# Where the polynomial's q and g's first part are made in the last block of the first MLP, and how wide the steps of a weight conversion are

## The chip, the cores and the metric

One core of a Trainium2 chip runs the whole program. The metric is the device time of one execution in microseconds (us); lower is better. Several executions are timed and their median counts; one more execution is taken with the hardware profiler.

## What is computed

The reference chains three parts. A recurrence with a 48 x 48 state per head (4 batches, 8 heads, 768 steps) gives 3072 tokens of width 384. The first MLP (384 to 2048 to 384) follows, and then a second MLP (384 to 1024 to 384) with a softmax-gated norm between its two products.

```python
x = attn_out.transpose(0, 2, 1, 3).reshape(3072, 384)
h = x @ w_in;  x = (h - np.tanh(h)) @ w_out               # first MLP
h = x @ w_in2; solu = h * softmax(h)                      # second MLP
out = ((solu - mean) / np.sqrt(var + 1e-06) * g_ln) @ w_out2
```

The weights come as 64-bit floats and are turned into 32-bit ones on the chip.

## The kernel before

Each 32-bit operand of the two MLPs is held as a rounded high part and a low part, so that one product takes three matmul passes (low by high, high by low, high by high).

**The first MLP** runs over 6 blocks of 512 tokens (index i, `NB` is 6) and, in each, over 16 tiles of 128 hidden columns (index m). I count the tiles through: tile s is block s // 16, so block 0 holds tiles 0 to 15 and the last block tiles 80 to 95. `part1` (line 328) makes one tile. Nine matmuls (L334) fill a PSUM bank `hp`; the pool of these has two banks, so the matmuls of tile s+2 need the bank of tile s free. Then h - tanh(h) is made as an odd polynomial: ScalarE squares hp into t (L339), VectorE makes y = hp * t (L340), ScalarE makes the inner square p from t (L342), VectorE finishes y (L344) from p and y, ScalarE raises a range flag from t and writes its unused main result to q (L345), y is rounded into g's first part (L347 on ScalarE or L349 on GpSimd), and GpSimd makes the second part, y minus the first (L350). In block 0 p is the bank hp itself and the rounding is ScalarE's L347; in the other blocks p is q, an SBUF tile, and the rounding is GpSimd's L349.

`part2` (line 353) takes g two tiles later: nine matmuls (L357) add it into three PSUM banks x2p. At the end of a block ScalarE copies these out (L362), and the result goes through DRAM to the second MLP.

**The conversion** (`convert`, line 109) turns a pair of 64-bit weight rows into 768 32-bit columns. ScalarE scales the low words (L118), VectorE shifts and masks the high words (L125), adds the sign bits (L126) and adds the low words (L127); ScalarE scales half by the norm's weights (L129, second MLP only) and rounds (L130), GpSimd makes the low part (L131). L125 and L126 run in two steps of 384 columns each. For the first MLP (`conv_a`, during block 0) the intermediate a lies in PSUM; for the second (`conv_b`, eight conversions, issued in the last block) there is no bank to spare, and a lies in the SBUF tile x, of which there are two buffers. `conv_b` of k is called at every second tile of the last block (line 551), but two of them start earlier and the rest is pulled ahead.

**Order.** The Python order is not the order on the engines: a planner sorts every engine's instructions by simulated time when the program is built. Each engine then runs its queue in that order, and an instruction that waits holds up all that stand behind it on its engine. Until the last block starts, the recurrence for later tokens is mixed into the same queues. After the last block the second MLP follows (L412, L446, L457); one half of its first product's weights is ready in the last block, and its first matmuls run there.

The lines that matter are quoted.

```python
p = hp if i == 0 else q                                   # L341
nc.scalar.activation(p, t, AF.Square, bias=..., scale=F_S)
v.scalar_tensor_tensor(y, p, F_E, y, ALU.add, ALU.mult)   # L344
```

Of the kernel before, what the change touches and what calls it, by code (L numbers as in the profile page):

```python
# [19 lines left out]
NT, DM, FF, FF2 = 3072, 384, 2048, 1024  # L20
# [5 lines left out]
NB = NT // BLK  # L26
# [29 lines left out]
class Kern:  # L56
# [52 lines left out]
    def convert(self, pool, raw, hi, lo, scale=None, bank=None):  # L109

        nc, v = self.nc, self.nc.vector
        flat = raw.rearrange("p i f two -> p (i f) two")
        H_, L_ = flat[:, :, 1], flat[:, :, 0]
        x = pool.tile([128, 2 * DM], U32, tag="cv_x", name="cv_x")
        xf = x.bitcast(F32)
        nc.scalar.activation(L_, L_, AF.Copy, scale=2.0**-29)  # L118
        for i in range(2):
            s = slice(i * DM, (i + 1) * DM)  # L120
            if bank is None:
                a = x[:, s]
            else:
                a = bank.tile([128, 4, C], F32, tag="a", name="cv_a").rearrange("p j t -> p (j t)")[:, 0:DM].bitcast(U32)
            v.tensor_scalar(a, H_[:, s], 3, 0x3FFFFFF8, ALU.logical_shift_left, ALU.bitwise_and)  # L125
            v.scalar_tensor_tensor(x[:, s], H_[:, s], 0xC0000000, a, ALU.bitwise_and, ALU.bitwise_or)  # L126
        v.tensor_tensor(x, x, L_, ALU.add)  # L127
        if scale is not None:
            nc.scalar.activation(xf[:, DM:], xf[:, DM:], AF.Copy, scale=scale)  # L129
        nc.scalar.copy(hi, xf)  # L130
        nc.gpsimd.tensor_tensor(lo, xf, hi, ALU.subtract)  # L131
# [196 lines left out]
    def part1(self, i, m):  # L328
        nc, v, g = self.nc, self.nc.vector, self.nc.gpsimd
        hp = self.ps_h.tile([128, BLK], F32, tag="h", name="hp")  # L330
        xs = self.xs[i % 2]
        seq = [(a, b, j) for j in range(KM) for a, b in ((1, 0), (0, 1), (0, 0))]
        for n, (a, b, j) in enumerate(seq):
            self.mm(hp, self.wa[:, a, m, j * 128:(j + 1) * 128], xs[:, b, j], start=n == 0, stop=n == len(seq) - 1)  # L334
        t = self.gp.tile([128, BLK], F32, tag="t", name="t")
        q = self.gp.tile([128, BLK], F32, tag="q", name="q")
        y = self.gp.tile([128, BLK], F32, tag="y", name="y")
        gs = self.gs.tile([128, 2, BLK], F32R, tag="g", name="g")
        nc.scalar.activation(t, hp, AF.Square)  # L339
        v.tensor_tensor(y, hp, t, ALU.mult)  # L340
        p = hp if i == 0 else q  # L341
        nc.scalar.activation(p, t, AF.Square, bias=self.c_fsb, scale=F_S)  # L342
        col = 2 * NU + i * NM + m
        v.scalar_tensor_tensor(y, p, F_E, y, ALU.add, ALU.mult)  # L344
        self.last_act = nc.scalar.activation(q, t, AF.Relu, bias=self.c_t2, accum_out=self.flags[:, col:col + 1])  # L345
        if i == 0:
            nc.scalar.copy(gs[:, 0], y)  # L347
        else:
            g.tensor_scalar(gs[:, 0], y, 1.0, 1.0, ALU.mult, ALU.mult)  # L349
        g.tensor_tensor(gs[:, 1], y, gs[:, 0], ALU.subtract)  # L350
        return gs
# [419 lines left out]
```

## Time and profile before

| what | us |
|---|---|
| median of 3 timed executions | 837.1 (836.93 to 837.52) |
| the profiled execution's own time | 833.47 |
| its span, first to last instruction | 831.7 |
| TensorE (PE) busy | 779.4 |
| VectorE (DVE) busy | 548.6 |
| ScalarE (ACT) busy | 490.5 |
| GpSimd (POOL) busy | 377.2 |

PE runs the matmuls, PEld loads their weights. Times in the trace count from the span's start. A row of the timeline gives the start, the length, the engine, the line, the operation, output and inputs, their shapes, how many instructions were merged into the row, and in brackets the idle time of the engine before it and what ended that. A granted clock of 1.00 is TensorE's full 2.4 GHz, 0.50 is 1.2 GHz. The last block's matmuls run from about 520 us to 603 us.

### The profile page before, as it was taken

How to read it: one execution, taken by the hardware profiler on the slowest of the kernel's cores; microseconds unless marked ns; L12 is line 12 of the kernel's file. 1: busy time of each engine (PE TensorE's matmuls, PEld its weight loads, DVE VectorE, ACT ScalarE, POOL GpSimd, SP SyncE). 2: the span in 40 equal slices, each digit the busy share in tenths (PEclk: the TensorE clock that was granted, in tenths of full speed). 3: DMA queues.
4: the chain of work that ended last, by engine and by line, in shares of the span. 5: the costliest groups of instructions: out<-in, count | busy, mean ns of one | idle time of the engine just before them, and what ended most of it. 6: DMA issues, size and time to landing. Idle time of an engine off the chain costs nothing.

```text
span 831.7 us, 13450 instructions
## 1 busy us (share of the span) xinstructions
PE 779.4 (94%) x4706; PEld 649.1 (78%) x4706; DVE 548.6 (66%) x997; ACT 490.5 (59%) x928; POOL 377.2 (45%) x360
## 2 busy tenths in 40 slices
PE   3778988999999999999999999889989999999996
PEld 2656766778878888888888788667879999999996
DVE  4688889666664566565556763895287577667763
ACT  3436776677666767677677765655445454445442
POOL 3544765655555655556556465676412111111110
PEclk9988998899999999999999999999999999999998
DMA  9966567435455554463434220410021111111101
GB/s 164 166 107 127 138 146 151 136 100 115 90 120 114 125 108 105 107 157 81 119 100 130 82 81 25 140 50 2 10 67 39 48 39 48 39 48 39 48 29 33
DMA packets 151309, 74.32 MB, mean 89 GB/s; under 512 B 107328, under 2 KB 142784, under 8 KB 151232
## 3 DMA queue, kind: packets, MB, share of 16 engines
q1 hardware_dynamic: 151232, 73.37, 37.0%
q8 instruction: 39, 0.64, 0.3%
q14 instruction: 38, 0.31, 0.1%
HBM read 61.54 MB, written 9.44 MB: 85 GB/s over the span
## 4 chain that ended last, share of the span: by engine, by line
PE 75%; DVE 11%; DMA 4%; issue 2%; POOL 2%; ACT 2%; SPq 2%; DVEq 0%; ACTq 0%; POOLq 0%
PE hp L334 19%; PE x2p L357 18%; PE o L457 12%; PE h L412 11%; PE qk L254 3%; PE tp L218 3%; DVE cv_x L126 2%; PE tt L446 2%; DVE cv_x L127 2%; PE y L296 2%; PE y L293 2%; DMA raw<-in_moe_w_out_dram 1%; DVE cv_x L125 1%; DMA raw<-in_moe_w_in_dram 1%; PE kt L260 1%
## 5 line engine op out<-in xcount | busy, mean ns | idle before, releaser
L357 PE MATMUL x2p<-g,wa 128*128 128x512 f32 x864 | 226.4, 401 | 9.0 <-POOL g L350 4.6
L334 PE MATMUL hp<-xs,wa 128*128 128x512 f32 x864 | 225.8, 403 | 6.7 <-POOL wa L131 3.2
L334 PEld LDWEIGHTS hp<-xs,wa 128*128 128x128 f32 x864 | 162.5, 192 | 45.2 <-POOL wa L131 3.7
L357 PEld LDWEIGHTS x2p<-g,wa 128*128 128x128 f32 x864 | 160.3, 191 | 46.0 <-POOL g L350 6.3
L350 POOL TENSOR_TENSOR g<-y,g 128x512 fp32r<-128x512 f32 x96 | 129.3, 1347 | 17.4 <-ACT g L347 9.7
L340 DVE TENSOR_TENSOR y<-hp,t 128x512 f32<-128x512 f32 x96 | 66.2, 689 | 106.6 <-ACT t L339 103.6
L457 PE MATMUL o<-wb,ts 128*128 128x384 f32 x576 | 110.0, 341 | 1.0 <-DVE ts L448 1.0
L345 ACT ACTIVATE q<-t,cst 128x512 f32<-128x512 f32 x96 | 69.5, 724 | 68.1 <-DVE y L344 67.8
L412 PE MATMUL h<-wb,x2s 128*128 128x512 f32 x432 | 103.8, 392 | 2.8 <-DVE so L432 2.4
L349 POOL TENSOR_SCALAR g<-y 128x512 fp32r<-128x512 f32 x80 | 53.9, 674 | 114.8 <-DVE y L344 111.4
L457 PEld LDWEIGHTS o<-wb,ts 128*128 128x128 f32 x576 | 100.5, 188 | 2.9 <-DVE ts L448 1.3
L412 PEld LDWEIGHTS h<-wb,x2s 128*128 128x128 f32 x432 | 80.6, 188 | 19.8 <-issue 3.0
L339 ACT ACTIVATE t<-hp 128x512 f32<-128x512 f32 x96 | 56.6, 591 | 44.8 <-PE hp L334 44.6
L437 POOL TENSOR_TENSOR st<-st,cst 128x1 f32<-128x1 f32 x24 | 13.5, 563 | 136.2 <-DVE st L436 134.8
L344 DVE SCALAR_TENSOR_TENSOR y<-q,y 128x512 f32<-128x512 f32 x80 | 65.4, 818 | 10.6 <-ACT q L342 5.6
L342 ACT ACTIVATE q<-t,cst 128x512 f32<-128x512 f32 x80 | 57.7, 722 | 2.0
L435 ACT ACTIVATE e<-so 128x1024 f32<-128x1024 f32 x24 | 25.4, 1059 | 49.4 <-DVE so L434 49.4
L425 DVE TENSOR_REDUCE st<-h 128x1 f32<-128x1024 f32 x24 | 29.4, 1224 | 28.6 <-PE h L412 27.1
L428 DVE TENSOR_REDUCE part<-e 128x32 f32<-128x1024 f32 x24 | 29.3, 1220 | 27.9 <-ACT e L427 27.9
L218 PE MATMUL tp<-ident,rkw 128*128 128x128 f32 x264 | 41.9, 292 | 6.0 <-DMA rkw<-in_w_dram 5.7
L402 POOL TENSOR_TENSOR x2s<-x2s 128x384 fp32r<-128x384 f32 x24 | 24.4, 1018 | 48.3 <-ACT x2s L401 40.0
L131 POOL TENSOR_TENSOR wa<-cv_x,wa 128x768 fp32r<-128x768 f32 x16 | 29.4, 1838 | 35.3 <-ACT wa L130 35.3
(114 smaller groups left out, 1211.1 us busy)
## 6 DMA issues: line engine op xcount, KB each, us to landing
raw<-in_moe_w_out_dram SPq DMA_DIRECT2D x48, 384.0 KB, 4.0
raw<-in_moe_w_in_dram SPq DMA_DIRECT2D x64, 144.0 KB, 3.2
raw<-in_moe_w_in_dram SPq DMA_DIRECT2D x16, 384.0 KB, 3.1
rkw<-in_w_dram SPq DMA_DIRECT2D x24, 192.0 KB, 4.3
rkw<-in_r_dram SPq DMA_DIRECT2D x24, 192.0 KB, 4.5
rkw<-in_k_dram SPq DMA_DIRECT2D x24, 192.0 KB, 3.9
vt<-in_v_dram SPq DMA_DIRECT2D x24, 192.0 KB, 4.4
x2d<-x2o SPq DMA_DIRECT2D x18, 256.0 KB, 2.2
```

The source lines that it names most:

```text
L218: self.nc.tensor.transpose(p[:, j], self.rkw[u % 2][:, i, 2 * j:2 * j + 2, :], self.ident)
L334: self.mm(hp, self.wa[:, a, m, j * 128:(j + 1) * 128], xs[:, b, j], start=n == 0, stop=n == len(seq) - 1)
L339: nc.scalar.activation(t, hp, AF.Square)
L340: v.tensor_tensor(y, hp, t, ALU.mult)
L342: nc.scalar.activation(p, t, AF.Square, bias=self.c_fsb, scale=F_S)
L344: v.scalar_tensor_tensor(y, p, F_E, y, ALU.add, ALU.mult)
L345: self.last_act = nc.scalar.activation(q, t, AF.Relu, bias=self.c_t2, accum_out=self.flags[:, col:col + 1])
L349: g.tensor_scalar(gs[:, 0], y, 1.0, 1.0, ALU.mult, ALU.mult)
L350: g.tensor_tensor(gs[:, 1], y, gs[:, 0], ALU.subtract)
L357: self.mm(self.x2p[d], self.wa[:, a, m, sl], gs[:, b], start=m == 0 and n == 0, stop=m == NM - 1 and n == 2)
L412: self.mm(p[:, f], xs[:, a, j], self.wb[:, b, 4 * f:4 * f + 4, j * 128:(j + 1) * 128], start=q == 0, stop=q == 8)
L457: self.mm(p, ts[:, a, k], self.wb[:, b, k, DM:], start=q == 0, stop=q == 3 * NM2 - 1)
```

## The change

In the last block, as in block 0 before, L342 writes its result into the bank hp in place of the SBUF tile q, L344 reads it from there, and g's first part is rounded by ScalarE (L347) in place of GpSimd (L349). In the conversion for the second MLP the two steps of 384 columns become one of 768: one L125 and one L126 in place of two of each. The conversion for the first MLP is unchanged.

```diff
-        for i in range(2):
-            s = slice(i * DM, (i + 1) * DM)
+        n = 1 if bank is None else 2
+        for i in range(n):
+            s = slice(i * 2 * DM // n, (i + 1) * 2 * DM // n)
             if bank is None:
-                a = x[:, s]
+                a = x
             else:
                 a = bank.tile([128, 4, C], F32, tag="a", name="cv_a").rearrange("p j t -> p (j t)")[:, 0:DM].bitcast(U32)
...
-        p = hp if i == 0 else q
+        ends = i in (0, NB - 1)
+        p = hp if ends else q
         nc.scalar.activation(p, t, AF.Square, bias=self.c_fsb, scale=F_S)
...
-        if i == 0:
+        if ends:
             nc.scalar.copy(gs[:, 0], y)
         else:
             g.tensor_scalar(gs[:, 0], y, 1.0, 1.0, ALU.mult, ALU.mult)
         g.tensor_tensor(gs[:, 1], y, gs[:, 0], ALU.subtract)
```

## Rows read from the trace of the kernel before

**Rows 1.** Busy by stretch: length, then PE, PEld, DVE, ACT, POOL, granted clock, DMA.

```profile
528.00:540.00 12.00, 9.04 (x35) 6.14 (x35) 11.76 (x12) 8.93 (x17) 8.51 (x6) 1.00 0.64 221
552.00:570.00 18.00, 13.99 (x51) 10.19 (x50) 14.89 (x16) 9.73 (x18) 13.19 (x11) 0.91 0.01 1
...
570.00:597.00 27.00, 27.00 (x120) 22.31 (x119) 10.47 (x15) 14.76 (x29) 13.59 (x15) 1.00 0.00 1
...
558.00:560.00 2.00, 2.00 (x6) 1.52 (x6) 2.00 (x2) 0.62 (x1) 2.00 (x2) 0.50 0.00 0
```

**Rows 2.** Waits of the matmuls by what ended them, 515 to 600 us.

```profile
PE x2p L357 <- POOL g L350: 4.4, 3, 3.2
```

**Rows 3.** Timeline of PE in the last block.

```profile
525.82 2.37 PE L334 MATMUL hp<-xs,wa 128*128 128x512 f32 x9
...
557.66 5.27 PE L357 MATMUL x2p<-g,wa 128*128 128x512 f32 x15 [3.19 <-POOL g L350]
563.23 2.33 PE L334 MATMUL hp<-xs,wa 128*128 128x512 f32 x9 [0.30 <-DVE y L340]
...
588.44 2.20 PE L334 MATMUL hp<-xs,wa 128*128 128x512 f32 x9
```

**Rows 4.** Timeline of DVE in the last block.

```profile
526.55 0.61 DVE L125 TENSOR_SCALAR cv_x<-raw 128x384 uint32<-128x384 uint32 x2
527.09 0.68 DVE L344 SCALAR_TENSOR_TENSOR y<-q,y 128x512 f32<-128x512 f32 x1
...
530.99 1.75 DVE L344 SCALAR_TENSOR_TENSOR y<-q,y 128x512 f32<-128x512 f32 x1
...
535.59 1.02 DVE L126 SCALAR_TENSOR_TENSOR cv_x<-raw,cv_x 128x384 uint32<-128x384 uint32 x2
536.74 0.96 DVE L127 CUSTOM_DVE_ANT_0 cv_x<-raw,cv_x 128x1536 uint16<-128x1536 uint16 x1
...
538.40 1.75 DVE L344 SCALAR_TENSOR_TENSOR y<-q,y 128x512 f32<-128x512 f32 x1
...
552.89 1.43 DVE L126 SCALAR_TENSOR_TENSOR cv_x<-raw,cv_x 128x384 uint32<-128x384 uint32 x2
...
555.72 2.11 DVE L125 TENSOR_SCALAR cv_x<-raw 128x384 uint32<-128x384 uint32 x2
...
563.28 0.69 DVE L344 SCALAR_TENSOR_TENSOR y<-q,y 128x512 f32<-128x512 f32 x1
...
584.01 0.69 DVE L344 SCALAR_TENSOR_TENSOR y<-q,y 128x512 f32<-128x512 f32 x1
```

**Rows 5.** Timeline of POOL in the last block.

```profile
537.75 1.85 POOL L131 TENSOR_TENSOR wb<-cv_x,wb 128x768 fp32r<-128x768 f32 x1 [2.30 <-ACT wb L130]
...
555.11 1.16 POOL L349 TENSOR_SCALAR g<-y 128x512 fp32r<-128x512 f32 x1 [1.66 <-DVE y L344]
556.24 2.72 POOL L350 TENSOR_TENSOR g<-y,g 128x512 fp32r<-128x512 f32 x2
```

**Rows 6.** Lines on their own: count, then min/median/max ns, first and last start.

```profile
L344 DVE SCALAR_TENSOR_TENSOR y<-q,y x80: 677/693/1752, 177.0 to 596.3; 128x512 f32<-128x512 f32 x80
...
L344 DVE SCALAR_TENSOR_TENSOR y<-hp,y x16: 673/682/692, 77.3 to 169.8; 128x512 f32<-128x512 f32 x16
...
L342 ACT ACTIVATE hp<-t,cst x16: 667/692/702, 76.6 to 169.0; 128x512 f32<-128x512 f32 x16
...
L347 ACT CAST g<-y x16: 600/616/632, 80.7 to 170.6; 128x512 fp32r<-128x512 f32 x16
...
L349 POOL TENSOR_SCALAR g<-y x80: 610/620/1184, 177.9 to 597.1; 128x512 fp32r<-128x512 f32 x80
```

**Rows 7.** Waits of the matmuls by what ended them, block 0, 76 to 176 us.

```profile
PE hp L334 <- DVE y L344: 2.7, 1, 2.7
PE x2p L357 <- ACT g L347: 2.4, 1, 2.4
```

**Rows 8.** Timeline of ACT in the last block.

```profile
548.29 0.62 ACT L129 ACTIVATE cv_x<-cv_x,gl 128x384 f32<-128x384 f32 x1 [4.56 <-DVE cv_x L127]
```

## The prediction

> **What bounds the kernel now.** I read the busy time by stretch first, because the change touches only the last block and the conversions that run in it. What a reader should see there is that TensorE has nearly no gaps where the last block runs alone (27.00 us busy of 27.00 from 570 to 597 us) and has gaps only while the conversions run beside it: 12.00 - 9.04 = 2.96 us from 528 to 540 and 18.00 - 13.99 = 4.01 us from 552 to 570 [rows 1]. From 540 to 552 it has none. That is 6.97 us of idle TensorE, and it is all that this change can win directly.
>
> A second loss hangs on the first. After the longest wait, 3.19 us, fifteen matmuls took 5.27 us [rows 3]; nine take 2.20 us elsewhere including the end of the last [rows 3], so fifteen would take about 3.6. The granted clock read 0.50 from 558 to 560 us, so the lower level of 1.2 GHz [rows 1]. That is about 1.7 us more. **The ceiling** of the change is thus 6.97 + 1.7 = 8.7 us.
>
> Then I read who ends the gaps: in 515 to 600 us the second-part subtraction on GpSimd, L350, ends 4.4 us of them, one of 3.2 us [rows 2]. Then I followed this one back on the engines' timelines. L350 of tiles 84 and 85 ran together only at 556.24, behind L349 of tile 85 at 555.11, which waited for VectorE's L344 of tile 85 [rows 5]. VectorE is what is full there: 11.76 of 12.00 us from 528 to 540 [rows 1]. Much of that is not work. L344 took 1.75 us twice, beginning at 530.99 and at 538.40, where its median is 0.693 [rows 4, 6]; the second of these began while GpSimd's L131 ran from 537.75 to 539.60, and lasted 0.55 us beyond it [rows 4, 5]. L125 of two steps took 2.11 us against 0.61, and L126 of two steps 1.43 us against 1.02 [rows 4]. So the chain is: VectorE is held while GpSimd runs, L344 comes late, g comes late, TensorE waits.
>
> **The change part by part.**
>
> *L344 reads hp.* The form that reads q and y, both in SBUF, goes up to 1752 ns; the form that reads hp never took over 692 ns in 16 instances, though fourteen conversions, each with its L131 on GpSimd, run in block 0 [rows 6]. So I take the stretch out of the two long ones: 2 x (1.75 - 0.69) = 2.1 us of VectorE's queue.
>
> *The rounding leaves GpSimd.* Sixteen L349 of 0.62 us [rows 6], 9.9 us, go from GpSimd and become sixteen L347 of 0.616 us, 9.9 us, on ScalarE. VectorE stood behind L349 in at least two places: L126 at 552.89 was 1.43 - 1.02 = 0.4 us longer, and L125 at 555.72 began 0.55 us before the L349 from 555.11 ended [rows 4, 5]. Together 1.0 us. On ScalarE there is room: it is busy 8.93 of 12.00 and 9.73 of 18.00 us in the two stretches [rows 1]. I cost its 9.9 us at nothing; the cover is this idle time, and what it costs when the cover is gone is a rival below.
>
> *Whole steps.* Two L126 of 384 columns took 1.02 us, and one pass over all 768 columns, L127, took 0.96 [rows 4]. A whole-step L126 is not in the trace; L127 is its nearest row, and the saving 0.06 us. For L125 I take the same. Six of the eight conversions have these steps in the last block (two are ahead of it): 6 x 2 x 0.06 = 0.7 us. The bounds are nothing, and 6 x (0.61 / 2 + 1.02 / 2) = 4.9 us if the length of a step did not depend on its columns at all; L127's row speaks for the small end.
>
> VectorE's queue is then shorter by 2.1 + 1.0 + 0.7 = **3.8 us**. As this queue is what sets g's time in the starved stretch, I take it as TensorE's gain one for one. The lower bound is zero (where what is released is held by the next GpSimd instruction instead), the upper one all 6.97.
>
> *The clock.* If the gap of 3.19 us gets shorter by most of this, the low clock after it should go too: **1.7 us**. The bounds are 0 and 1.7, and a new gap of this length elsewhere would make it 0.
>
> *The added order: L342 after L340.* L342 may write hp only once L340 has read it, so L342, which ran beside L340, now follows it and adds up to 0.69 us [rows 6] to the time from hp to g. Behind this wait on ScalarE's queue stand the next tile's t and the conversion's L129 and L130. Where TensorE is not starved it is hidden: L344 of tile 92 ended at 584.70, and the matmuls of tile 94, which take the same bank, began at 588.44 [rows 3, 4], so 3.7 us are left. At the last tile it can cost between 0 and 0.7 us. I take 0.
>
> *The bank is held longer.* Now tile s+2 may fill hp once L340 of tile s has read it; after the change it needs L344 of tile s, which stands behind conversion steps in VectorE's queue. With the order and times of before this would put off hp seven times, from tile 82 (began 525.82; L344 of tile 80 ended at 527.77, 1.95 us later) to tile 88 (began 563.23; L344 of tile 86 ended at 563.97, 0.74 us later) [rows 3, 4], 13.1 us over the seven. That is the upper bound; it counts no reordering and no other matmul in the gaps. The lower one is zero. Block 0 is the nearest row, for it runs this very form beside fourteen conversions, and there TensorE waited once for L344 in front of L334, for **2.7 us** [rows 7]. I take that.
>
> The sum is 3.8 + 1.7 - 2.7 = 2.8 us. The profiled execution would go from 833.47 to 830.7 us. It lies 3.6 us below the median of the timed executions; the difference carries over, so I forecast 837.1 - 2.8 = **834.3 us**, and for this case itself 832 to 835.4.
>
> **The rivals.**
>
> *The bank wait decides (slower).* Between L340 and L344 VectorE now has a gap, as it waits for L342, and a conversion step is ready to be put there. Such a step lasts up to 2.11 us when GpSimd holds it [rows 4], and it is whole, so L344 comes late, and both banks are held. The point from which it decides is the 3.7 us of room [rows 3, 4]: two such steps between L340 and L344 use it up. If half of the 13.1 us stays, the sum is 3.8 - 6.5 with no clock back: 839.8 us; if all, up to 846 less what the gaps of before overlap with, 6.97, or about 840 again. For it: VectorE was full in this stretch. Against it: block 0 shows it once in 16 tiles, and the planner knows of the bank. Chance 0.20.
>
> *The wait moves to ScalarE (no change).* ScalarE's queue is held by L129, which waits for VectorE's L127; at 548.29 that was 4.56 us [rows 8]. If L347 of a tile stands behind such a wait, g's first part comes late by the time that is left of it. Block 0 shows TensorE waiting for L347 once, 2.4 us [rows 7]. One wait of 4.56 us eats the 3.8 us and leaves the clock low: 837.1 - 3.8 + 4.56 = 837.9, less when it is partly hidden; with 2.4 us, 835.7. I give 837.0. Chance 0.18.
>
> *Whole steps hold GpSimd (no change).* L349 at 555.11 lasted 1.16 us against a median of 0.62, while VectorE's L125 began beside it [rows 4 to 6]: VectorE and GpSimd hold up each other. A whole L126 lasts 0.45 us longer than a half (0.96 against 0.51), a whole L125 by about 0.3. Over six conversions, and with GpSimd busy 71 in 100 of the time (8.51 of 12.00, [rows 1]), this is 6 x 0.75 x 0.71 = 3.2 us of GpSimd's queue: 834.3 + 3.2 = 837.5 us if all of it ends up in g. Against it: GpSimd has just lost 9.9 us. Chance 0.05.
>
> The Trainium skill's page "SBUF — State Buffer", section "Who interferes with whom", says that VectorE and GpSimd share one pair of SBUF ports, given as a lock for a whole instruction, to a VectorE instruction with two SBUF inputs or in a two-port mode; so by it the whole steps keep the lock longer, and L125 and L126, which stay in SBUF, go on being held. By that rule the gain of the polynomial's part stays and this rival is what the second part of the change does; the trace agrees for the form that reads hp (0.692 us at most), and no row shows a whole step.
>
> *All of it comes back.* Without L349 on GpSimd, L350 of tile 84 no longer stands behind tile 85's rounding (555.11 to 556.27, [rows 5]), and if the other gaps go as well, the sum is the ceiling: 837.1 - 8.7 = 828.4, with parts of it 830 or 831. Chance 0.13.
>
> *That the change does not do what it says*, that is, that L344 is held for another reason than its second SBUF input, would take 2.1 us from the sum: 836.4, no change. The sixteen instances of at most 692 ns speak against it, and it is in the chances of no change.
>
> **How the numbers follow.** The forecast's chance is 0.44, all back 0.13, no change 0.23 (0.18 and 0.05), slower 0.20. About 0.2%, or 1.7 us, is what a measurement of this kernel can tell from no change. So faster is 0.57, same 0.23, slower 0.20. The range, 829.0 to 839.5, leaves out about half of the fullest gain and half of the slower case.
>
> **What would show it.** In the profile of the changed kernel L344 of the last block should be at most 0.70 us in all sixteen tiles. The gaps of TensorE between 520 and 570 us should be about 4 us, with L350 no longer the largest of what ends them and L334 waiting for L344 a few times. The last conversion should be done some 4 us earlier. The clock should stay at 1.00 after the gaps. I am wrong if a gap of over 3 us in front of L334 is ended by L344, or one in front of L357 by L347; and where the planner has put the conversions in quite another place the whole sum has to be made anew.

## The result and the profile after

The changed kernel was timed in three series beside the kernel before. Its median was 830.3 us against 837.3 in the first, a ratio of 0.9918 with a 95% interval of 0.9893 to 0.9942; 831.9 against 835.1 in the second (0.9952, 0.9936 to 0.9969); and 831.0 against 835.0 in the third (0.9952, 0.9933 to 0.9971). It is faster, by 0.5 to 0.8%. Gains in us are here the ratio applied to the median before: 6.9 us in the first series and 4.0 in each of the two later ones, which hold more executions. The medians themselves differ by 7.0, 3.2 and 4.0 us. The forecast was 2.8 us.

The lines stand one or two further down the file than before: the L334, L340, L342, L344, L347, L349 and L350 of the text above are L335, L341, L344, L346, L349, L351 and L352 in the changed kernel, and L125 to L127 are L126 to L128, L357 is L359, L412 is L414.

**One trace is not one time.** The profiled executions' spans are 831.7 us before and 830.8 after, only 0.9 us apart. To see why, I cut each trace at the last block's first matmul and at the second MLP's first matmul behind it. The rows are the timeline of TensorE, of the kernel before and then of the changed one.

```profile
519.46 0.84 PE L334 MATMUL hp<-xs,wa 128*128 128x512 f32 x3
...
603.77 4.38 PE L412 MATMUL h<-wb,x2s 128*128 128x512 f32 x18 [0.47 <-ACT x2o L362]
```

```profile
521.44 0.84 PE L335 MATMUL hp<-xs,wa 128*128 128x512 f32 x3
...
602.78 4.38 PE L414 MATMUL h<-wb,x2s 128*128 128x512 f32 x18 [0.25 <-ACT x2o L364]
```

The last block took 603.77 - 519.46 = 84.3 us before and 602.78 - 521.44 = 81.3 after: 3.0 us less. What lies behind it took 227.9 and 228.0 us. The changed execution had lost 2.0 us before the last block began, where the order of the instructions is the same but for a few neighbours and the whole steps of the two early conversions. Over the fourteen traces of this case the time to block 1 alone, which no edit touches, went from 168.6 to 173.2 us. So from here on I compare the last block, not the span.

Busy time by stretch, after (columns as in [rows 1]):

```profile
528.00:540.00 12.00, 9.23 (x38) 6.97 (x39) 8.28 (x11) 10.38 (x20) 6.33 (x4) 1.00 0.59 197
540.00:552.00 12.00, 10.32 (x44) 7.86 (x43) 10.87 (x12) 10.15 (x19) 7.21 (x4) 1.00 0.38 131
552.00:570.00 18.00, 17.23 (x67) 13.73 (x68) 10.52 (x12) 12.25 (x23) 10.51 (x7) 0.91 0.04 12
570.00:597.00 27.00, 27.00 (x121) 22.38 (x120) 8.69 (x13) 17.66 (x33) 9.13 (x8) 1.00 0.00 1
```

VectorE is no longer full from 528 to 540 us (8.28 of 12.00, against 11.76 in [rows 1]), and the large gap of TensorE between 552 and 570 is gone (0.77 us against 4.01). New is idle time of 1.68 us between 540 and 552; most of it belongs to a gap of 1.96 us that ends at 552.65. From 528 to 540 TensorE idles nearly as long as before, 2.77 us against 2.96, although VectorE has room there. The waits of the matmuls in the last block, after:

```profile
PE hp L335 <- DVE y L346: 4.7, 3, 2.4
PE x2p L359 <- ACT g L349: 0.5, 1, 0.5
```

GpSimd's second part, which ended 4.4 us of the gaps before [rows 2], ends none. In its place stands the wait for the bank. Where VectorE's time went is seen in its groups in 70 us of the last block, before and then after (busy us, mean ns of one, idle time before):

```profile
L126 DVE SCALAR_TENSOR_TENSOR cv_x<-raw,cv_x 128x384 uint32<-128x384 uint32 x12 | 13.2, 1136 | 0.0
L344 DVE SCALAR_TENSOR_TENSOR y<-q,y 128x512 f32<-128x512 f32 x14 | 12.9, 924 | 1.5 <-ACT q L342 0.6
L125 DVE TENSOR_SCALAR cv_x<-raw 128x384 uint32<-128x384 uint32 x12 | 10.5, 912 | 4.0 <-POOL wb L131 4.0
L127 DVE CUSTOM_DVE_ANT_0 cv_x<-raw,cv_x 128x1536 uint16<-128x1536 uint16 x6 | 7.1, 1190 | 0.4
```

```profile
L346 DVE SCALAR_TENSOR_TENSOR y<-hp,y 128x512 f32<-128x512 f32 x14 | 9.6, 687 | 7.8 <-ACT hp L344 7.8
L128 DVE CUSTOM_DVE_ANT_0 cv_x<-raw,cv_x 128x1536 uint16<-128x1536 uint16 x6 | 8.7, 1454 | 0.2
L127 DVE SCALAR_TENSOR_TENSOR cv_x<-raw,cv_x 128x768 uint32<-128x768 uint32 x6 | 8.2, 1372 | 0.1
L126 DVE TENSOR_SCALAR cv_x<-raw 128x768 uint32<-128x768 uint32 x6 | 6.0, 1006 | 6.4 <-POOL wb L132 6.4
```

I call **held time** what an instruction lasts beyond the shortest of its kind in the same stretch, summed over the stretch. Before, it is 12 x (1136 - 545) ns for L126, 12 x (912 - 347) for L125, 14 x (924 - 677) for L344 and 6 x (1190 - 944) for L127: 7.1 + 6.8 + 3.5 + 1.5 = 18.8 us. After, it is 2.6 for L127 (shortest 944), 2.8 for L126 (547), 3.0 for L128 (948) and 0.1 for L346: 8.5 us.

**The low clock.** The gap of 1.96 us after has such a stretch behind it as the gap of 3.19 us had before. The rows are busy time by stretch; the seventh number is the granted clock:

```profile
553.00:554.00 1.00, 1.00 (x5) 0.81 (x4) 0.96 (x3) 1.00 (x3) 0.62 (x1) 0.71 0.00 0
554.00:555.00 1.00, 1.00 (x4) 0.81 (x3) 1.00 (x1) 0.67 (x1) 1.00 (x2) 0.50 0.00 0
555.00:556.00 1.00, 1.00 (x3) 0.75 (x3) 0.86 (x2) 0.00 (x0) 1.00 (x1) 0.50 0.00 0
556.00:557.00 1.00, 1.00 (x4) 0.81 (x3) 1.00 (x1) 0.60 (x1) 1.00 (x1) 0.59 0.00 0
```

It costs 0.29 + 0.50 + 0.50 + 0.41 = 1.7 us, as much as the one before. I take 1.7 us off per stretch to compare the last blocks **at full clock**: 82.6 us before and 79.6 after.

### The profile page after: what moved, and what is told of

Read it like the earlier page. It is cut to its first block, busy times and chain, and to the rows that moved or that the text cites. A ratio compares the mean times of both kernels' runs of the same rounds, so it can differ in the third digit from the quotient of the medians.

```text
span 830.8 us, 13425 instructions
## 1 busy us (share of the span) xinstructions
PE 778.7 (94%) x4706; PEld 649.5 (78%) x4706; DVE 537.6 (65%) x981; ACT 499.8 (60%) x944; POOL 365.3 (44%) x344
## 4 chain that ended last, share of the span: by engine, by line
PE 78%; DVE 8%; DMA 4%; ACT 3%; issue 3%; SPq 2%; POOL 2%; DVEq 0%; ACTq 0%; POOLq 0%
PE hp L335 21%; PE x2p L359 19%; PE o L459 12%; PE h L414 11%; PE qk L255 3%; PE tp L219 3%; PE tt L448 2%; PE y L297 2%; PE y L294 2%; DMA raw<-in_moe_w_out_dram 2%; DVE cv_x L128 1%; DVE cv_x L127 1%; PE kt L261 1%; PE ds L271 1%; DMA raw<-in_moe_w_in_dram 1%
## 5 line engine op out<-in xcount | busy, mean ns | idle before, releaser
L335 PE MATMUL hp<-xs,wa 128*128 128x512 f32 x864 | 226.8, 405 | 11.0 <-DVE y L346 7.2
L359 PE MATMUL x2p<-g,wa 128*128 128x512 f32 x864 | 225.1, 399 | 4.8 <-ACT g L349 3.8
L335 PEld LDWEIGHTS hp<-xs,wa 128*128 128x128 f32 x864 | 163.8, 193 | 49.4 <-DVE y L346 6.5
L359 PEld LDWEIGHTS x2p<-g,wa 128*128 128x128 f32 x864 | 159.6, 190 | 40.4 <-ACT g L349 4.7
L352 POOL TENSOR_TENSOR g<-y,g 128x512 fp32r<-128x512 f32 x96 | 128.3, 1337 | 59.0 <-ACT g L349 44.7
L341 DVE TENSOR_TENSOR y<-hp,t 128x512 f32<-128x512 f32 x96 | 66.2, 689 | 107.4 <-ACT t L340 103.8
L414 PE MATMUL h<-wb,x2s 128*128 128x512 f32 x432 | 104.0, 393 | 1.6 <-DVE so L434 1.4
L347 ACT ACTIVATE q<-t,cst 128x512 f32<-128x512 f32 x96 | 69.5, 724 | 53.5 <-DVE y L346 52.9
L414 PEld LDWEIGHTS h<-wb,x2s 128*128 128x128 f32 x432 | 80.6, 188 | 18.6 <-issue 1.8
L340 ACT ACTIVATE t<-hp 128x512 f32<-128x512 f32 x96 | 56.6, 591 | 44.4 <-PE hp L335 44.1
L351 POOL TENSOR_SCALAR g<-y 128x512 fp32r<-128x512 f32 x64 | 42.6, 666 | 89.3 <-DVE y L346 81.5
L346 DVE SCALAR_TENSOR_TENSOR y<-q,y 128x512 f32<-128x512 f32 x64 | 51.1, 799 | 9.3 <-ACT q L344 5.3
L429 ACT ACTIVATE e<-h,st 128x1024 f32<-128x1024 f32 x24 | 26.8, 1115 | 34.7 <-DVE st L428 34.0
L344 ACT ACTIVATE q<-t,cst 128x512 f32<-128x512 f32 x64 | 46.1, 722 | 1.6
L132 POOL TENSOR_TENSOR wa<-cv_x,wa 128x768 fp32r<-128x768 f32 x16 | 29.4, 1838 | 34.8 <-ACT wa L131 34.8
```

Of the source, the lines that this page charges most:

```text
L359: self.mm(self.x2p[d], self.wa[:, a, m, sl], gs[:, b], start=m == 0 and n == 0, stop=m == NM - 1 and n == 2)
L414: self.mm(p[:, f], xs[:, a, j], self.wb[:, b, 4 * f:4 * f + 4, j * 128:(j + 1) * 128], start=q == 0, stop=q == 8)
```

## The experiments

The kernel before, the change and the twelve further runs in one table. The ratio is to the kernel before, timed beside it. "Low" counts the stretches at 1.2 GHz in the last block of the one trace; "gaps" are TensorE's idle us in it; "held" is VectorE's held time in 70 us of it.

| run | ratio (95% interval) | last block | low | at full clock | gaps | held |
|---|---|---|---|---|---|---|
| before | 1 | 84.3 | 1 | 82.6 | 7.4 | 18.8 |
| the change (first trace) | 0.9918 (0.9893 to 0.9942) | 81.3 | 1 | 79.6 | 5.5 | 8.5 |
| after_again | 0.9952 (0.9936 to 0.9969) | 81.3 | 1 | 79.5 | 5.3 | 8.5 |
| after_third | 0.9952 (0.9933 to 0.9971) | 81.4 | 1 | 79.7 | 6.3 | 8.3 |
| poly_only | 0.9963 (0.9950 to 0.9976) | 82.5 | 2 | 79.1 | 5.4 | 9.5 |
| steps_only | 0.9971 (0.9956 to 0.9987) | 81.6 | 0 | 81.6 | 7.4 | 15.7 |
| bank_only | 1.0016 (1.0002 to 1.0030) | 85.4 | 1 | 83.7 | 9.4 | 12.1 |
| round_only | 1.0000 (0.9985 to 1.0015) | 82.6 | 1 | 80.9 | 7.1 | 12.5 |
| shift | 0.9992 (0.9976 to 1.0008) | 85.2 | 2 | 81.8 | 7.8 | 18.8 |
| own_bank_only | 0.9973 (0.9957 to 0.9990) | 83.0 | 2 | 79.6 | 6.3 | 14.1 |
| own_bank | 0.9897 (0.9873 to 0.9920) | 77.3 | 0 | 77.3 | 3.5 | 7.8 |
| conv_bank_hp | 0.9916 (0.9895 to 0.9937) | 79.6 | 0 | 79.6 | 5.6 | 6.4 |
| conv_bank_only | 0.9885 (0.9860 to 0.9910) | 76.5 | 0 | 76.5 | 2.4 | 8.7 |
| conv_bank | 0.9876 (0.9847 to 0.9905) | 75.8 | 0 | 75.8 | 1.8 | 9.6 |

**The change again.** The kernel is the changed one.

> The changed kernel once more, for a second profile and a second series of times. I cut each trace in three: from the start to the last block's first L335 (the line is L334 in the kernel before), from there to the second MLP's first matmul behind the last x2o (the last block), and the rest. In the first traces the last block took 84.3 us before and 81.3 us after, a gain of 3.0, while the medians of the timed executions differ by 7.0. Theory 1: the last block alone carries the gain and the rest is how one execution differs from another ahead of it, so the times differ by 3 to 5 us when more of them are taken and the last block is 81 to 82 us again. Theory 2: something outside the last block got faster too, so the times differ by 7 again and the first or the last cut of this trace is some 4 us shorter than in the kernel before (519.5 and 227.9 us).

> The changed kernel a third time, for the size of its gain (0.9918 and 0.9952 of the kernel before in two series) and for the low clock behind its gaps. Theory 3: the last block takes 79.5 us at full clock again, with one or two stretches at the lower clock behind the gaps of 2.4 and 1.9 us or none, so that it lies between 79.5 and 83 us; the time is 3 to 7 us below the kernel before. Rival (the first series was chance): below 2 us.

The last block is 81.3 and 81.4 us again, the first cut 524.0 and 521.3 us against 519.5 before, and the last 227.7 in both. So nothing outside the last block got faster; theory 1's reading holds. Both time differences are 4.0 us by the ratio (3.2 and 4.0 by the medians), within the 3 to 5 that it gave.

**The two parts of the diff, each alone.** For poly_only the conversion goes back to two steps, for steps_only the polynomial back to the kernel before.

```diff
-        n = 1 if bank is None else 2        # poly_only
+        n = 2
...
-        ends = i in (0, NB - 1)             # steps_only
+        ends = i == 0
```

> Only the polynomial's part of the change: q in hp's bank and the rounding on ScalarE in the last block; the conversion keeps its two steps. Theory 1 (VectorE's queue is held by GpSimd at L344 and behind the rounding): nearly all of the gain stays, the last block takes 81.5 to 82.5 us and the time is within 1 us of the whole change. Rival (the whole steps carry the gain, as the rest pays for its own bank wait): the last block takes 83.5 us or more and the time is within 2 us of the kernel before.

> Only the whole steps in the second MLP's conversion; the polynomial as in the kernel before. Theory 1: 0.7 us of VectorE's queue, so the last block takes 83.5 to 84.3 us and the time is within 1 us of the kernel before. Rival: whole steps carry the gain, the last block takes 82 us or less. Second rival (a whole step holds GpSimd for longer): the last block takes 85 to 88 us and the time is 1 to 3 us above the kernel before.

Each part alone gives most of the gain: 3.1 and 2.4 us of time, against 4.0 together. The polynomial's part did as theory 1 said: the last block took 82.5 us with two low stretches, which is 3.5 us less than before at full clock. For the steps theory 1 failed: the last block took 81.6 us, under the 82 that the rival named, and the time fell by 2.4 us and not by less than 1. Of the 2.7 us that the block got shorter, 1.7 are the low stretch that this trace does not have; at full clock 1.0 us is left, little more than the 0.8 by which a mere change of order moves the block (the run shift, below). The rival by which whole steps hold GpSimd is seen, but not as a loss: GpSimd's second part (L352) took 1.56 us on average, against 1.38 for L350 before. The waits of the matmuls and VectorE's third step in steps_only:

```profile
PE hp L335 <- DVE y L341: 4.7, 3, 2.5
PE x2p L359 <- POOL g L351: 1.3, 1, 1.3
```

```profile
L128 DVE CUSTOM_DVE_ANT_0 cv_x<-raw,cv_x 128x1536 uint16<-128x1536 uint16 x6 | 12.7, 2121 | 0.4
```

L128, which the edit does not touch, is now the one that is held, 2.1 us each against 1.19 before. So held time partly moves from one instruction to another: L128 has 5.5 us more of it, and the sum falls from 18.8 to 15.7 us only.

**The polynomial's two halves.** bank_only keeps L349's rounding to block 0, round_only keeps p = hp to block 0; both have the conversion of before.

```diff
-        if ends:                            # bank_only
+        if i == 0:
             nc.scalar.copy(gs[:, 0], y)
...
-        p = hp if ends else q               # round_only
+        p = hp if i == 0 else q
```

> Only q in hp's bank in the last block; the rounding stays on GpSimd (L351), the conversion in two steps. Theory 1: VectorE is no longer held at L346 (at most 0.70 us each), worth 2.1 us of its queue, less 2.7 us for the bank that is held longer; GpSimd still has its sixteen roundings, so the last block takes 83 to 85 us and the time is 0 to 2 us below the kernel before. Rival (the rounding's move is nothing, what counts is L346's form): the last block takes 81.5 us, as with the whole change.

> Only g's first part rounded by ScalarE in the last block; q stays in SBUF, the conversion keeps its two steps. In the runs so far the last block took, with the low-clock stretches taken out, 82.6 us before, 79.6 with the whole change, 79.1 with the polynomial's part alone, 83.7 with only q in hp's bank, where the matmuls waited 7.5 us for L346. Theory 2 (formed on these): the bank costs more than L346's form gives, and the rounding's move off GpSimd carries the gain. Then this run has at most 1 us of waits of L335 for L346, the last block takes 78.5 to 80.5 us at full clock, and the time is 2.5 to 5 us below the kernel before. Theory 1 (as predicted: L346's form and the rounding together): L346 is still stretched to 1.7 us, the last block takes 81 to 82.5 us and the time is 0 to 2 us below.

Neither gives anything alone in time, and bank_only is slower, by 0.16%, with an interval that just excludes 1. Theory 1 took it for 0 to 2 us faster and fails there. Theory 2, formed after it, made the rounding the carrier; it fails too, as round_only is no faster in time, and its last block, 80.9 us at full clock, is longer than the 78.5 to 80.5 that theory 2 gave. The matmuls' waits in bank_only, and VectorE ahead of one of them:

```profile
PE hp L335 <- DVE y L346: 7.5, 4, 2.9
PE x2p L359 <- POOL g L351: 0.9, 1, 0.9
```

```profile
545.66 3.77 DVE L127 SCALAR_TENSOR_TENSOR cv_x<-raw,cv_x 128x384 uint32<-128x384 uint32 x2
549.56 1.81 DVE L128 CUSTOM_DVE_ANT_0 cv_x<-raw,cv_x 128x1536 uint16<-128x1536 uint16 x1
551.29 0.68 DVE L341 TENSOR_TENSOR y<-hp,t 128x512 f32<-128x512 f32 x1
...
553.97 0.69 DVE L346 SCALAR_TENSOR_TENSOR y<-hp,y 128x512 f32<-128x512 f32 x1 [0.52 <-ACT hp L344]
```

L346 itself is at its shortest. But it stands in the queue behind conversion steps that GpSimd holds, and now two banks wait for it: the matmuls began again at 554.71, after 2.45 us of idling. In round_only no matmul waits for L346, but L346 is stretched again (mean 0.87 us), and the matmuls wait for L341 and for a late g:

```profile
PE hp L335 <- DVE y L341: 4.4, 3, 2.2
PE x2p L359 <- POOL g L352: 2.5, 1, 2.5
```

Added up, the halves give 0.6 us at full clock (1.1 lost and 1.7 won), but together, in poly_only, 3.5. So each needs the other. In poly_only the matmuls wait 2.9 us for L346, against 7.5 in bank_only, and VectorE's held time is 9.5 us against 12.1; that the rounding on GpSimd holds the steps ahead of L346, and that its move shortens the bank wait in this way, fits these numbers but has no run of its own.

**Is it only the order?** In shift the conversion is called at odd tiles, and nothing else differs from the kernel before.

```diff
-        if 0 <= s - LAST < NM and (s - LAST) % 2 == 0:
+        if 0 <= s - LAST < NM and (s - LAST) % 2 == 1:
```

> The kernel before with nothing changed but the place of the conversion's calls: at every odd tile of the last block in place of every even one. The same instructions, in another order. Rival theory (the planner's order alone makes such differences, whatever is changed): the last block moves by more than 1.5 us at full clock from its 82.6. Theories 1 and 2: within 1 us of it, and the time within 1.5 us of the kernel before.

The time is the same to 0.1%, and the last block differs by 0.8 us at full clock. So this change of the order does not make the gain. That every order would do as little is not shown by one run, and a difference of 0.8 us between the traces of two kernels can come from the order alone.

**The form of L346 without the bank.** own_bank and own_bank_only put p from tile 81 on into another PSUM bank, the one that the second MLP's output product uses later (tag "o"). The first is otherwise the changed kernel, the second the kernel before. (The text ahead of the prediction says that there is no bank to spare for the second conversion. From the last block on there is one, this bank.)

```diff
-        p = hp if ends else q
+        p = hp if i == 0 else q if i < NB - 1 else hp if m == 0 else self.ps_o.tile([128, BLK], F32, tag="o", name="pq")
...
             ps_r = pool(R2, "ps_r", side="right", space=PSUM)
+            K.ps_o = ps_r
```

> The whole change, but from tile 81 on p of the polynomial lies in a PSUM bank of its own (the one that the second MLP's output product uses later) and hp is free once L341 has read it. Theory 2: the 4.7 us that L335 waited for L346 with the whole change go, so TensorE's gaps in the last block are 1 to 3 us, it takes 77 to 78.5 us at full clock and the time is 4 to 6 us below the kernel before. Rival (VectorE's queue is the limit and the bank only shows it): the waits turn to L359 for g, the last block takes 79 to 80 us as with the whole change, and the time is 3 to 4 us below the kernel before.

> As with only q in hp's bank, but from tile 81 on p lies in a PSUM bank of its own; the rounding stays on GpSimd and the conversion in two steps. Theory 3 (from the runs so far: the held time of VectorE falls alike with every part, 18.8 us before to 12.1 with only the bank, and the bank wait of 7.5 us is what took it back): without that wait the last block takes 78 to 80.5 us at full clock, against 83.7 with hp's bank, and the time is 2 to 5 us below the kernel before. Rival (the planner's order made that run slow, not the bank): the last block stays above 82 us, the time within 1.5 us of the kernel before.

Against bank_only, own_bank_only differs in the bank alone and is 4.1 us shorter at full clock (79.6 against 83.7). Its matmuls wait for L341, not for L346:

```profile
PE hp L335 <- DVE y L341: 5.8, 3, 2.7
```

With the rest of the change, own_bank takes 77.3 us at full clock, as theory 2 gave, and 2.3 us less than the change. Its time, 0.9897 of the kernel before, is 8.6 us lower where 4 to 6 were expected, and its gaps are 3.5 us where 1 to 3 were. So **the price of the held bank is real and was 2 to 4 us**, and this change pays it. The times agree: by the ratios own_bank_only is 3.6 us faster than bank_only.

**Taking VectorE's conversion out of GpSimd's way.** In conv_bank and conv_bank_only the conversion's a lies in that idle bank, in two steps. The file is one line longer again: L127 to L129 are here L125 to L127 of the kernel before, and L336, L342, L347, L350, L353 and L360 are its L334, L340, L344, L347, L350 and L357. conv_bank has ScalarE's rounding and q in SBUF, conv_bank_only the polynomial of before, conv_bank_hp that of the change.

```diff
-        self.convert(pool, raw, self.wb[:, 0, k], self.wb[:, 1, k], self.gl[:, k:k + 1])
+        self.convert(pool, raw, self.wb[:, 0, k], self.wb[:, 1, k], self.gl[:, k:k + 1], bank=self.ps_o)
```

> The rounding on ScalarE, q of the polynomial in SBUF, and the second MLP's conversion in two steps with its intermediate a in that other PSUM bank, as the first MLP's conversion has it. Theory 2 with VectorE held by GpSimd mostly in the conversion: L126 and L127 are at most 0.57 us each where in the kernel before they go to 2.0 us, the last block takes 77 to 79 us at full clock, and the time is 4 to 6 us below the kernel before. Rival (what counts is how many instructions VectorE has between two of the polynomial's): two conversions can no longer begin before the last block's bank exists and each has five VectorE instructions in place of three, so the last block takes 80 us or more and the time is 0 to 3 us below.

> Only the intermediate a of the second MLP's conversion in the idle bank; the polynomial is that of the kernel before, with q in SBUF and the rounding on GpSimd. Theory 3: of the 18.8 us that VectorE was held in the last block 13.9 were at the two lines that a touches; without them the last block takes 77 to 79 us at full clock and the time is 4 to 8 us below the kernel before, more than the whole change gives. Rival (the rounding's move is needed too): the last block takes 80 us or more and the time is 0 to 3 us below.

> The whole change and a in the idle bank in two steps, so that L126, L127 and L346 all have one SBUF input. Theory 3: nothing but L128 is held any more; if the bank hp costs its wait, the last block takes 76 to 77.5 us at full clock and the time is 7 to 10 us below the kernel before, no better than a in the bank with q in SBUF (75.8 us). Rival (the bank wait came only from late VectorE instructions): it takes 75.5 us or less and is the fastest of all.

VectorE's groups in conv_bank, and what its matmuls wait for in the last block:

```profile
L128 DVE SCALAR_TENSOR_TENSOR cv_x<-raw,cv_a 128x384 uint32<-128x384 uint32 x13 | 7.1, 549 | 2.4 <-POOL wb L133 2.2
L127 DVE TENSOR_SCALAR cv_a<-raw 128x384 uint32<-128x384 uint32 x12 | 6.6, 553 | 0.1
```

```profile
PE x2p L360 <- ACT g L350: 0.6, 1, 0.6
PE hp L336 <- DVE y L342: 0.4, 1, 0.4
```

The two conversion lines are never held (mean 553 and 549 ns, where the kernel before had 912 and 1136 for the same columns), and no gap of the last block reaches 1 us. conv_bank is the fastest of all: 824.7 us against 834.8, a ratio of 0.9876, which beats both kernels. The theory's size fell short, 4 to 6 us against 10.4; conv_bank_only shows that this one edit gives 9.6 us of it by itself, without the rounding, where 4 to 8 were expected. One thing beside the bank differs in these runs: the first two conversions, whose L127 starts at 467 and 475 us in the kernel before, start with the bank, and the same line runs at 517 and 521 us. What this shift gives or costs has no run of its own. conv_bank_hp was to be the test of the bank wait, and it is plainer than I had expected (79.6 us, where 76 to 77.5 were given): with almost nothing held but L129, giving p the bank hp costs 3.8 us at full clock against conv_bank, 79.6 against 75.8, and 3.3 us of time, with 2.8 us of waits for L347 and 1.5 for the rounding. It has less held time than conv_bank, 6.4 us against 9.6, and is the slower one: the sum of held time does not rank the kernels, and what counts is whether a matmul waits for it.

```profile
PE hp L336 <- DVE y L347: 2.8, 2, 1.6
PE x2p L360 <- ACT g L350: 1.5, 1, 1.5
```

## Why the prediction was right, and where its steps were not

The direction, the stretch and the mechanism were right: the gain lies in the last block, VectorE's queue was held by GpSimd there, and the bank takes a part back. The traces' 3.0 us stand beside my 2.8. The medians of the three series, 830.3, 831.9 and 831.0 us, lie inside the range, but all below the 832 to 835.4 that I gave for this case itself (in the two later series the kernel before was 2 us lower as well, at 835.1 and 835.0). That the sum came out near the traces is luck: two of its terms were wrong and cancelled. 3.8 + 1.7 - 2.7 was, by the traces, 5.3 + 0 - 2.3. The 5.3 is what own_bank gains and the 2.3 what separates it from the change, so that these two leave 3.0 by the way they are taken and prove nothing by their sum.

- *L344 reads hp* (2.1 us). No instance of the last block is over 0.693 us, as expected. The stretch that went was 3.5 us, since I had counted only two instances.
- *The rounding leaves GpSimd* (1.0 us) and *whole steps* (0.7 us). What a whole step itself saves was right: in the timelines L126 and L127 last 0.55 and 0.95 us where two halves took 0.61 and 1.02. Mis-sized was what GpSimd holds: the held time of the conversion's three lines fell from 15.4 to 8.4 us, where I had counted two rows by eye. Together with L344 the held time fell by 10.3 us, while my whole release was 3.8. The rows that would have shown it were there: the means of the four groups against their shortest.
- *One for one.* This step failed. With the whole change but without the held bank (own_bank), the held time is 11.0 us less than before, and the last block 82.6 - 77.3 = 5.3 us shorter at full clock. So what VectorE's release is worth is 5.3 us, where I had 3.8, and it is half of what was released. The rest was released where no matmul waited for it. This is my reading of the difference; one sign of it is that VectorE after the change sits idle for 6.4 us before L126, until GpSimd's L132, and for 7.8 before L346, until the L344 that the change itself put in front of it.
- *The bank held longer* (2.7 us). The mechanism was there and the size near: own_bank and the change differ by 2.3 us at full clock. By the other pairs the price is 4.1 (own_bank_only) and 3.8 (conv_bank_hp), so the one row from block 0 was a fair guide. The matmuls' waits for L346 themselves are longer, 4.7 to 6.1 us in three traces of the change.
- *The clock* (1.7 us). This failed in the traces: all three of the change have one low stretch in the last block, as the trace before has. I had tied it to the length of one gap. In the same kernel a gap of 1.96 us had one behind it in the first trace, and the gap of 1.95 us at the same place in after_third had none. In the timed executions it is not shown to be nothing: their mean granted clock was 0.973 before (68 executions) and 0.977 after (17), and the one trace of the kernel before, with 0.979, is above its mean. If all of that difference fell where the matmuls set the time, it would be 0.0045 x 835 = 3.7 us, an estimate; where it fell is not on record. bank_only had 0.979 and was slower, so the clock alone does not set the time.
- *ScalarE at nothing* held for this change: from 570 to 597 us no matmul waits for anything, and the one wait for its rounding was 0.5 us. It is not free everywhere: in poly_only and conv_bank_hp one wait for the rounding lasted 1.5 us. The added order of L344 after L341 did cost nothing where TensorE is fed (27.00 of 27.00).
- *The rivals.* The bank wait does end on the other side when it comes without the rest: bank_only is 0.16% slower. Its upper bound I had misread: the seven rows add up to 15.3 us in the trace, not 13.1, and an eighth tile adds 1.0. The room of 3.7 us is used up as I wrote it, by steps between L341 and L346. In the change this is the gap at 552.65 (timeline of VectorE and of TensorE):

```profile
546.15 0.69 DVE L341 TENSOR_TENSOR y<-hp,t 128x512 f32<-128x512 f32 x1 [1.06 <-ACT t L340]
546.84 1.64 DVE L126 TENSOR_SCALAR cv_x<-raw 128x768 uint32<-128x768 uint32 x1
548.51 2.49 DVE L127 SCALAR_TENSOR_TENSOR cv_x<-raw,cv_x 128x768 uint32<-128x768 uint32 x1
551.03 0.96 DVE L128 CUSTOM_DVE_ANT_0 cv_x<-raw,cv_x 128x1536 uint16<-128x1536 uint16 x1
551.91 0.68 DVE L346 SCALAR_TENSOR_TENSOR y<-hp,y 128x512 f32<-128x512 f32 x1
...
552.65 3.58 PE L335 MATMUL hp<-xs,wa 128*128 128x512 f32 x9 [1.96 <-DVE y L346]
```

The planner put a whole conversion between the two, and it took 5.1 us where its three steps last 2.4 at their shortest. The longest gap of the change, 2.36 us (at the same place in all three traces), is another case:

```profile
523.93 2.19 DVE L126 TENSOR_SCALAR cv_x<-raw 128x768 uint32<-128x768 uint32 x1 [4.00 <-POOL wb L132]
526.16 0.96 DVE L127 SCALAR_TENSOR_TENSOR cv_x<-raw,cv_x 128x768 uint32<-128x768 uint32 x1
527.03 0.68 DVE L341 TENSOR_TENSOR y<-hp,t 128x512 f32<-128x512 f32 x1
...
529.57 0.68 DVE L346 SCALAR_TENSOR_TENSOR y<-hp,y 128x512 f32<-128x512 f32 x1
...
530.30 2.35 PE L335 MATMUL hp<-xs,wa 128*128 128x512 f32 x9 [2.36 <-DVE y L346]
```

Here L341 itself is late, as it stands behind a conversion that waited 4.00 us for GpSimd's L132 and was then held; what lies between L341 and L346 runs at its shortest. Before the change the same wait of 4.00 us stood there, but the matmuls needed L340 only and idled 0.24 us. This one gap is most of what TensorE still idles from 528 to 540 us.

The other rivals: *all of it comes back* had named 830 or 831 us, and the three medians come near it, but the traces do not bear it out, as 5.3 to 6.3 of the 7.4 us of gaps are left. *The wait moves to ScalarE* is the 0.5 us above. *Whole steps hold GpSimd* shows in the means of steps_only, without a loss.

Of the signs that I named, L346 stayed at or under 0.693 us, GpSimd's second part ends no gap, L335 waits for L346 three times and no gap exceeds 3 us. The last conversion is done 5.2 us earlier, counted from the start of the last block, where I had said some 4. The gaps from 520 to 570 us are 5.3 us and not about 4, and the clock did not stay at 1.00.

The Trainium skill's page "SBUF — State Buffer", section "Who interferes with whom", says that a VectorE instruction with at most one SBUF input and outside the two-port modes does not contend with GpSimd; the traces agree in every form tried here: L346 with p in PSUM stayed at or under 0.693 us, and the conversion's lines with a in PSUM at or under 0.561.

**What stays open.** The times differ by 4.0 us in two series and by 6.9 in the first, the traces by 3.0. One execution may lose another number of low stretches than the next, at 1.7 us each, and the traces of shift, poly_only and own_bank_only have two. If the kernel before lost two on average and the kernels without such stretches none, conv_bank would gain 82.6 - 75.8 + 3.4 = 10.2 us, conv_bank_only 9.5, own_bank 8.7 and conv_bank_hp 6.4, where 10.4, 9.6, 8.6 and 7.0 were timed. That fits, and the granted clocks on record lean the same way: 0.976 to 0.980 on average for these four kernels, against 0.973 before. But it is an estimate from one trace each. What decides whether a gap is followed by a low stretch I did not separate, nor why round_only, 1.7 us shorter at full clock, gains nothing in time; three gaps of 1.9 to 2.5 us in its trace would allow more low stretches than the one seen.

## What to carry to other kernels

When two engines hold each other, sum the held time of each group (its mean against its shortest) before costing an edit, then ask which matmul waits for it; here about half of what was released was worth anything. An intermediate that is moved to PSUM to free an engine should go to a bank that nobody waits for: the same form cost 2 to 4 us in the bank that the next matmuls fill, and the idle bank was worth most where the held time was, in the conversion. And compare the stretch that was changed, not the span, when executions differ by more ahead of it than the change gives.

## What the runs showed of the hardware

- Held time can move on to the next instruction in the queue: with whole steps alone the mean of L128, untouched, went from 1.19 to 2.12 us.
- A form that is slower by itself won: L125 takes 0.347 us at its shortest with a in SBUF and 0.547 with a in PSUM (conv_bank_only), but 0.912 and 0.552 on average beside GpSimd. With a in PSUM for L125 and L126 the kernel was 9.6 us faster.
- The length of a gap alone did not decide on the low clock: a stretch at 1.2 GHz followed gaps of 1.96 and 3.19 us, and in poly_only two of 1.47 and 0.59 us close together, and none followed one of 2.46 us in steps_only. In the changed kernel a gap of 2.36 us at one place had none behind it in the first trace and had one in after_third. The kernels whose largest gap in the last block was 1.75 us (own_bank), 1.59 (conv_bank_hp) or under 1 us (conv_bank, conv_bank_only) had none there.
